# Attention followed by a routed expert layer on one core: rows stored unnormalized and scaled after the gather, and the second search's steps placed by hand between expert 0's row tiles

## The chip, the cores and the metric

One NeuronCore of a Trainium2 chip runs the whole program. The metric is the device time of that core in microseconds (us); lower is better. PE is TensorE, DVE VectorE, ACT ScalarE, POOL GpSimd, SP SyncE (here only a DMA queue).

## The reference

```python
scores = q @ k.T / sqrt(64)                      # q, k, v: [8 batches, 8 heads, 576, 64]
scores = where(scores >= max(scores) - tau, scores, -1e9)
x = softmax(scores) @ v                          # -> 4608 rows of 512
logits = x @ w_gate                              # [4608, 8]
for tok, e in all (token, expert) pairs, largest logit first:
    if tok is unassigned and expert e has < 576 rows: assign tok to e
out[rows of e] = relu(x[rows of e] @ w1[e]) @ w2[e]     # w1 [512, 1024], w2 [1024, 512]
```

## The kernel before, in words

**Attention** (`attention`, L23 to L320) runs pairs of heads through scores, threshold, exponential, transposes and the product with v. It leaves, batch by batch, an unnormalized transposed result XT and a table of 1/denominator (`RD[b]`, one factor for each row and head). A unit `xt_unit(b,c)` (L201) turns one tile of 128 tokens back into rows: four PE transposes into one of two PSUM banks (tile `xo`, L205), an eviction into an SBUF row tile with the factors multiplied in, and a DMA on SP's queue into the DRAM tensor `xrows` [4608, 512], from which the experts gather. Batches 0 and 1 (10 units) are evicted during attention by one DVE multiply (L212). The other 30 units stand in the list `late` and run after attention: in 24 of them ACT copies PSUM to SBUF and POOL multiplies in place (both L218); the six with c = 4 take eight small ACT operations with the factor as scale (L216).

**The router** finds for one expert after another the logit at which it has its 576 rows. A search has seven levels: DVE compares all logits with a set of thresholds (`cmp`), PE counts by nine small matmuls (L420), DVE casts the counts (`cn`), PE folds them (L426), DVE compares with 576 (`jka`), PE reduces (L436 or L441), DVE forms the next thresholds (`E`). Then `pick` chooses the expert (L463), `rank` numbers its rows (L479, L480), and `pack` (L555) makes the list `idx` of its 576 rows: DVE one-hots, nine matmuls (L504), sixteen (L510), DVE `ih` and `idx`. `close` (L517) bars the assigned tokens and the full expert before the next search. All router operations on DVE are recorded through the planner `Vec` and show as line L358. `warm` (L525) emits 20, 4 and 50 matmuls that compute nothing in the first `pack`.

**The experts** (`moe`, L574): for expert number r of the order found, `w1_load` and `w2_load` bring the weights and split each into a high part (ACT, `w1h`, `w2h`) and a rest (DVE, `w1l`, `w2l`); `rows` (L626) issues five indirect DMAs on POOL's queue (L632), for each tile of rows four PE transposes (`turn` in the later kernel; L642), ACT writes `xh` (L645), DVE `xl`. `ffn` (L653) runs layer 1 (L662: eight output blocks f, each with 12 pairs of matmuls), ReLU on ACT (L668) and its split (`H`), layer 2 (L682), and scatters the rows (L689).

**What orders the work.** Each engine executes its list in the order in which the program is recorded. In attention the order is written out; during the first search the loop below puts one late unit about every 1.05 us between the search steps; from the first expert on, `run` steps generators (`packing`, the searches, loads, `rows`) by modelled times while `ffn` emits the matmuls. LATS, GA, RW are such modelled delays: of the search steps, from gather to first transpose, and between the row tiles. Expert 0's rows are transposed before its layer 1; those of experts 1 to 7 are transposed while PE works through layer 2 of the expert before.

```python
    while late:
        if nxt<=at:
            now=R.V.now=nxt; nxt=now+next(ph,1e6)
        else:
            now=at; late.pop(0)()(); at=now+XTY
```

Of the kernel before, what the change touches and what calls it, by code (L numbers as in the profile page):

```python
# [9 lines left out]
F32 = mybir.dt.float32  # L10
# [8 lines left out]
S=576; D=64; HS=288; QK=3*HS+2*S  # L19
PPB=8; LTB=1; VTB=5; HOLD=1; CAPV=3.3; RATE=(2.4,2.4); NBO=2; XAC=(4,); NDEF=4; XTB=4; XTY=1.05; XT0=2.0; XRB=2  # L20


def attention(ctx, tc, qk, vl, tau, wgd, xrows, xts, Lg, nb_batches, ident, swap, R, after_first):  # L23
# [338 lines left out]
class Router:  # L362
# [148 lines left out]
    def compact2(s,ps):  # L511
# [4 lines left out]
        return idx  # L516
    def close(s):  # L517
        V=s.V; wk=s.wk; L=s.L

        cl=wk.tile([128,8],F32,name="cl"); V.tensor_scalar(cl,s.k("w8"),s.m,-FMAX/2,op0=ALU.is_equal,op1=ALU.mult)  # L520
        V.tensor_tensor(L,L,cl.unsqueeze(1).to_broadcast([128,NC_,8]),op=ALU.add)
        u=wk.tile([128,NC_],F32,name="u"); V.tensor_scalar(u,s.sc,BIGS,-FMAX/2,op0=ALU.is_ge,op1=ALU.mult)
        u2=wk.tile([128,NC_],F32,name="u2"); V.scalar_tensor_tensor(u2,s.sc,BIGS+CAP,u,op0=ALU.is_lt,op1=ALU.mult)
        V.tensor_tensor(L,L,u2.unsqueeze(2).to_broadcast([128,NC_,8]),op=ALU.add)
    def warm(s,n):  # L525

        ps=s.ps()
        for i in range(n): s.T.matmul(ps[:,256:384],s.ones,s.tri,start=True,stop=True)
    def phase(s,last=False):
# [24 lines left out]
        held(0.2); s.rank2()  # L554
    def pack(s,first):  # L555
# [11 lines left out]
        yield V.wait() if first else 0.35  # L567
# [4 lines left out]
W1Y=5.0; L2O=(0,4,1,2,3); L2Z=1; HFB=3; RW=[0.2,0.6,1.0,2.0]; LOWP=(0,1); LPF=7; LOWT=1.4; PREPW=1; WLY=(1.0,1.0)  # L572

def moe(ctx,tc,R,start,xrows,w1,w2,out,ident):  # L574
# [10 lines left out]
    def w1_load(r,s):  # L585
        while r>0 and ("w1",r-1) not in done: yield 0.5
# [7 lines left out]
        s["w1h"]=w1p.tile([128,4,F],F32R,name="w1h"); s["w1l"]=w1p.tile([128,4,F],F32R,name="w1l")  # L594
        for k in range(4):
            t=s["w1s",k]
            if r==0:
                A.activation(s["w1h"][:,k],t,AF.Copy)
                while "idx" not in s: yield 0.25
                V.tensor_tensor(s["w1l"][:,k],t,s["w1h"][:,k].bitcast(F32),op=ALU.subtract)  # L600
                yield 1.1; continue
# [6 lines left out]
        done.add(("w1",r))  # L608
    def w2_load(r,s):
# [16 lines left out]
    def rows(r,s):  # L626
        while r>0 and ("x",r-1) not in done: yield 0.5
        order=(4,0,1,2,3) if r<=HALF else range(5)
        for t in order:
            n=128 if t<4 else 64  # L630
            x=wk.tile([128,D],F32,name="xg",bufs=5); s["xg",t]=x
            G.indirect_dma_start(out=x[:n],out_offset=None,in_=xrows,in_offset=IOA(ap=s["idx"][:n,t:t+1],axis=0))  # L632
        s["ei2"]=wk.tile([128,1],I32,name="ei2",bufs=2); G.tensor_copy(s["ei2"],s["ei"])
        done.add(("g",r))
        yield GA[min(r,3)]
        while r>0 and ("l1",r-1) not in done: yield 0.5
        s["xh"]=wk.tile([128,4,576],F32R,name="xh"); s["xl"]=wk.tile([128,4,576],F32R,name="xl")
        for t in order:
            n=128 if t<4 else 64
            ps=pt.tile([128,4,128],F32,name="pt")  # L640
            held[0]+=0.5
            for d in range(4): T.transpose(ps[:,d,:n],s["xg",t][:n,d*128:(d+1)*128],ident[:n,:n])  # L642
            if t<4: xv=lambda n: s[n][:,:,128*t+32*(t//2):128*t+32*(t//2)+128]; pv=ps
            else: xv=lambda n: s[n].rearrange("p k (a b) -> p k a b",a=2)[:,:,:,256:288]; pv=ps[:,:,:64].rearrange("p k (a b) -> p k a b",a=2)
            A.activation(xv("xh"),pv,AF.Copy)  # L645
            yield 0.8
            V.tensor_tensor(xv("xl"),pv,xv("xh").bitcast(F32),op=ALU.subtract)
            done.add(("row",r,t))
            if t==1: done.add(("half",r))
            yield RW[min(r,3)]  # L650
        done.add(("x",r))

    def ffn(r,s):  # L653
        H=wk.tile([128,8,2*CAP],F32R,name="H")
        for f in range(8):
            ps=pf.tile([128,2,512],F32,name="pf")
            for hs in (((0,),(1,)) if r<=HALF and f==0 else ((0,1),)):
                if hs==(1,): yield None
                for k in range(4):
                    for j,(w,x) in enumerate((("w1h","xh"),("w1h","xl"),("w1l","xh"))):  # L660
                        for h in hs:
                            T.matmul(ps[:,h,:HS],s[w][:,k,f*128:(f+1)*128],s[x][:,k,h*HS:(h+1)*HS],  # L662
                                     start=(k==0 and j==0),stop=(k==3 and j==2))
                        if not (k==3 and j==2): yield 0.125*len(hs)
            two=lambda a: a.rearrange("p (a b) -> p a b",a=2)
# [30 lines left out]
    def place():  # L696
        for r in range(8):
# [4 lines left out]
            def steps(g):  # L702
# [11 lines left out]
            yield from steps(start[0] if r==0 else R.phase(r==7))  # L714
            if r==0:
                yield from packing(r,s)
                yield 2.3; R.close(); yield 1.4
            else:
                if r<7: R.close()
                jobs.append([clk[0],packing(r,s)])  # L720
                yield 0.1
    def packing(r,s):
        for d in R.pack(r==0):
            held[0]+=R.pe; R.pe=0.0
            yield d
            V.now=clk[0]
# [88 lines left out]
```

## Time and profile before

| | |
|---|---|
| device time, median of 3 runs | 1034.47 us (1034.33 to 1034.84) |
| the profiled execution | 1035.17 us, span of its instructions 1033.4 us |
| PE busy | 979.6 us (95%), 9104 matmuls |
| DVE / ACT / POOL busy | 776.3 / 640.3 / 324.3 us |
| mean granted PE clock | 0.979 of full speed |
| first search, `idx` of expert 0 written | from 491 us to 535.6 us |
| expert 0, layer 1 complete | 584.6 us |

The busy shares are averages over three parts: attention (to about 490 us), the first search with expert 0's preparation (490 to 560), and the experts (to 1033). Matmuls are pipelined, so two rows of one engine may overlap by a little.

### The profile page before, as it was taken

The page shows a single profiled execution, that of the slowest core. Times are in us where ns is not written, and L with a number is a line of the kernel's source. Part 1 is how long each engine was busy: PE and PEld are TensorE (multiplying, and loading weights), DVE is VectorE, ACT ScalarE, POOL GpSimd, SP SyncE. Part 2 cuts the span into 40 slices and gives each one's busy share as a digit, 9 for nine tenths or more (in the row PEclk, how much of TensorE's full clock was granted, in tenths as well). Part 3 has the DMA queues.
Part 4 walks back from the last instruction along what each step waited for, and adds up shares of the span by engine and source line. Part 5 has one row for each costly group of instructions (what it writes and reads, how often), then busy time and mean ns, then how long its engine had stood idle before and what let it go on. Part 6 is the DMA issues. An engine that isn't in the chain of part 4 may idle for free. (4 is left out here: it accounts for less than half of the span.)

```text
span 1033.4 us, 24026 instructions
## 1 busy us (share of the span) xinstructions
PE 979.6 (95%) x9104; PEld 713.4 (69%) x9104; DVE 776.3 (75%) x2085; ACT 640.3 (62%) x1221; POOL 324.3 (31%) x485
## 2 busy tenths in 40 slices
PE   6999999999999999999668899999999999999996
PEld 3555555555555555555557779788897978889895
DVE  6999999999999999997677677757585676744230
ACT  5898888888888888886544335444352534445340
POOL 2333433333333343331653445312204021231201
PEclk9999999999999999999778999999999999999998
DMA  6222143243432222302463251504325051363101
GB/s 224 99 67 102 61 141 119 98 144 113 153 108 107 89 75 104 108 2 93 168 208 110 82 169 48 196 29 132 129 83 168 14 194 65 126 228 126 41 11 41
DMA packets 35715, 113.03 MB, mean 109 GB/s; under 512 B 4368, under 2 KB 4752, under 8 KB 35088
## 3 DMA queue, kind: packets, MB, share of 16 engines
q1 hardware_dynamic: 28496, 89.47, 24.4%
q0 software_dynamic: 5888, 18.88, 5.9%
q10 hardware_dynamic: 1216, 3.15, 0.9%
q8 instruction: 72, 1.18, 0.5%
q14 instruction: 43, 0.35, 0.1%
HBM read 89.19 MB, written 21.23 MB: 107 GB/s over the span
## 5 line engine op out<-in xcount | busy, mean ns | idle before, releaser
L75 POOL TENSOR_SCALAR nb<-nb,taub 128x1 f32<-128x1 f32 x288 | 147.3, 512 | 296.6 <-DVE z L74 252.4
L74 DVE TENSOR_SCALAR_CACHE_REDUCE z<-sc 128x576 f32<-128x576 f32 x288 | 205.9, 751 | 34.5 <-PE sc L69 33.0
L85 ACT ACTIVATE pp<-z,nb 128x576 f32<-128x576 f32 x256 | 187.4, 773 | 34.6 <-DVE z L74 33.2
L89 DVE SCALAR_TENSOR_TENSOR pp<-z,nb,pp 128x576 f32<-128x576 f32 x256 | 199.8, 812 | 0.3
L682 PE MATMUL pf<-w2h,H 128*128 128x512 f32 x576 | 196.1, 402 | 1.1 <-DVE H L358 1.1
L69 PE MATMUL sc<-qk 64*128 64x288 f32 (+1 forms) x1280 | 181.3, 428 | 6.5 <-DMA qk<-qk_dram 6.2
L144 PE MATMUL xo<-pt,vt 128*64 128x288 f32 x1024 | 151.9, 418 | 0.7 <-ACT xt L151 0.7
L113 ACT ACTIVATE pt<-tb 128x512 f32<-128x512 f32 x256 | 140.1, 594 | 13.8 <-PE tb L98 11.5
L98 PEld LDWEIGHTS tb<-ident,pp 64*128 64x128 f32 x2304 | 85.7, 139 | 71.8 <-ACT pt L113 16.8
L682 PE MATMUL pf<-w2l,H 128*128 128x512 f32 x320 | 128.2, 401 | 0.0
L689 POOL DMA_INDIRECT out_dram<-y,idx x40 | 42.7, 1067 | 265.1 <-ACT y L685 167.9
L682 PEld LDWEIGHTS pf<-w2h,H 128*128 128x128 f32 x576 | 106.3, 188 | 20.0 <-DVE H L358 1.5
L69 PEld LDWEIGHTS sc<-qk 64*128 64x128 f32 (+1 forms) x1280 | 94.3, 179 | 36.4 <-DVE pp L89 9.2
L98 PE MATMUL tb<-ident,pp 64*128 64x64 f32 x2304 | 108.8, 229 | 10.3 <-ACT pt L113 6.2
L662 PE MATMUL pf<-xh,w1h 128*128 128x288 f32 x512 | 113.4, 300 | 1.2 <-ACT xh L645 1.2
L662 PE MATMUL pf<-xh,w1l 128*128 128x288 f32 x512 | 113.7, 300 | 0.0
L662 PE MATMUL pf<-xl,w1h 128*128 128x288 f32 x512 | 113.1, 299 | 0.0
L668 ACT ACTIVATE hf<-pf 128x576 f32<-128x576 f32 x64 | 41.8, 652 | 105.3 <-PE pf L662 94.3
L144 PEld LDWEIGHTS xo<-pt,vt 128*64 128x64 f32 x1024 | 62.5, 136 | 63.5 <-issue 26.5
L685 ACT ACTIVATE y<-pf 128x512 f32<-128x512 f32 x40 | 23.9, 598 | 115.9 <-PE pf L682 99.3
L662 PEld LDWEIGHTS pf<-xh,w1h 128*128 128x128 f32 x512 | 82.9, 189 | 3.7 <-ACT xh L645 1.7
L662 PEld LDWEIGHTS pf<-xl,w1h 128*128 128x128 f32 x512 | 82.6, 189 | 0.2 <-DVE xl L358 0.2
(182 smaller groups left out, 1361.0 us busy)
## 6 DMA issues: line engine op xcount, KB each, us to landing
qk<-qk_dram SPq DMA_DIRECT2D x31, 1008.0 KB, 4.9
w2s<-w_dram SPq DMA_DIRECT2D x32, 512.0 KB, 6.0
w1s<-w_dram SPq DMA_DIRECT2D x28, 512.0 KB, 5.3
vt<-vl_dram SPq DMA_DIRECT2D x32, 320.0 KB, 5.5
xrows<-pp SPq DMA_DIRECT2D x24, 256.0 KB, 2.0
xts<-xt SPq DMA_DIRECT2D x2, 1152.0 KB, 5.2
pt<-xts SPq DMA_DIRECT2D x2, 1152.0 KB
xrows<-xr SPq DMA_DIRECT2D x8, 256.0 KB, 2.1
```

Source lines behind the costliest of these rows:

```text
L69: T.matmul(sc[o,f,:HS], kd["q",h][r,c], kd[k,h][r,:],start=True,stop=True)
L74: V.tensor_scalar(z,SC.pop(t)[:,:,:HS],-0.125,None,op0=ALU.mult,op1=ALU.min,accum_out=nb[:,0:1])
L75: G.tensor_scalar(nb[:,1:2],nb[:,0:1],taub[:,0:1],None,op0=ALU.add)
L85: A.activation(pview(t),ZB[t].rearrange("p a b -> p (a b)"),AF.Exp,bias=NBI[t][:,0:1],scale=-1.0)
L89: V.scalar_tensor_tensor(pv,ZB.pop(t).rearrange("p a b -> p (a b)"),NBI[t][:,1:2],pv,op0=ALU.is_le,op1=ALU.mult,accum_out=den_of(p)[:,p%4, ...
L98: g=slice(64*r,64*r+64); T.transpose(o[:,r],x[g],ident[g,g])
L113: A.activation(PT[p][:,i%2,:,(i//2)*128:(i//2+1)*128].rearrange("p k (r q) -> p r k q",r=2),tb,AF.Copy)
L144: T.matmul(xo[64*h:64*h+64,:HS],v[:,u,64*h:64*h+64],PT[p][:,h,u,q],start=(u==0),stop=False,skip_group_check=True)
L662: T.matmul(ps[:,h,:HS],s[w][:,k,f*128:(f+1)*128],s[x][:,k,h*HS:(h+1)*HS], start=(k==0 and j==0),stop=(k==3 and j==2))
L668: A.activation(hf,ps[:,:,:HS],AF.Relu)
L682: T.matmul(ps[:,0,:],H[:,f,c:c+128],s[w][:,f],start=(f==0 and j==0),stop=e)
L689: G.indirect_dma_start(out=out,out_offset=IOA(ap=s["idx"][:n,t:t+1],axis=0),in_=y[:n],in_offset=None)
```

## The change

1. `xrows` rows become 520 wide: 512 unnormalized values and the row's eight factors. An early unit is a DVE copy and a POOL operation of 128x8 for the factors (both L213 of the new file); a late unit is an ACT copy and an ACT copy of the factors (L215). The POOL multiplies and the small ACT operations of L216 are gone.
2. After the gather, DVE multiplies each row tile in place by its factors (`xg<-xg`); for tile 4 of expert 0 ACT does it in eight operations. The scale of an expert's first tile is recorded at the moment of its first transpose, that of each other tile one tile ahead.
3. For expert 0 the steps of the second search are written by hand between the row tiles; `close` is split into two parts inside `pack` (experts 0 and 1); `w1l` of expert 0 is written after the row tiles in column pieces; its layer 1 takes the products with `w1h` first.
4. The constants LATS, GA and RW change.

```diff
-            if b<nb_batches-NDEF-NBO: V.tensor_tensor(xv,pv,src,op=ALU.mult)
-            elif c in XAC:
...
+            if early:
+                V.tensor_copy(xv,ps[:n]); G.tensor_scalar(fv,src,1.0,0.0,op0=ALU.mult,op1=ALU.add)
             else:
-                A.activation(xv,pv,AF.Copy); G.tensor_tensor(xv,xv,src,op=ALU.mult)
+                A.activation(xv,ps[:n],AF.Copy); A.activation(fv,src,AF.Copy)
             nc.sync.dma_start(xrows[b*S+c*128:b*S+c*128+n,:],xr[:n])
...
         poh=s.onehot(prb); R=s.rank3(hib)
         if first: s.warm(WARM[0])
+        if alone: s.close1()
         yield V.wait()
         held(0.7); s.compact(cps,poh,R)
         if first: s.warm(WARM[1])
+        if alone: s.close2()
...
-LATS=[0.15,0.05,0.4]+[0.6]*5; FIX=(0.125,0.2)
-GA=[7.0,5.5,7.5,9.0]; HALF=1; WARM=[20,4,50]
+LATS=[0.15,0.12,0.25]+[0.35]*5; FIX=(0.125,0.2)
+GA=[5.0,6.0,7.0,7.0]; HALF=1; WARM=[20,4,50]
...
+        if r==0:
+            for k in range(4):
+                A.activation(s["w1h"][:,k],s["w1s",k],AF.Copy); yield 1.1
+            done.add(("w1",0))
+            for a,b in ((0,1),(1,2),(2,4),(4,8)):
+                while ("row",0,1 if a==0 else 3) not in done: yield 0.1
+                o=slice(128*a,128*b)
+                for k in range(4):
+                    V.tensor_tensor(s["w1l"][:,k,o],s["w1s",k][:,o],s["w1h"][:,k,o].bitcast(F32),op=ALU.subtract)
...
+        def scale(t):
...
+            if (r,t)==(0,4):
+                x=s["xg",t][:n]
+                for h in range(8): A.activation(x[:,64*h:64*h+64],x[:,64*h:64*h+64],AF.Copy,scale=x[:,D+h:D+h+1])
+                return
+            v=s["xg",t][:n,:D].rearrange("p (h d) -> p h d",h=8)
+            V.tensor_tensor(v,v,s["xg",t][:n,D:XW].unsqueeze(2).to_broadcast([n,8,64]),op=ALU.mult)
...
+            step(); scale(4); step(); scale(0); turn(4); step(); turn(0); step(); scale(1); low(4); step()
+            turn(1); low(0); step(2); scale(2); yield V.ease()
+            low(1); done.add("ahead"); yield 1.5
+            turn(2); yield 0.8
+            scale(3); low(2); yield 0.7
+            turn(3); low(3)
+            done.add(("x",0)); return
+        scale(order[0])
+        for i,t in enumerate(order):
+            turn(t)
+            if i<4: scale(order[i+1])
+            yield 0.8
+            low(t)
             yield RW[min(r,3)]
...
+                ops=[(k,j) for j in range(3) for k in range(4)] if r==0 else [(k,j) for k in range(4) for j in range(3)]
...
+                    if r==0 and (k,j)==(0,2): yield ("w1l",f)
```

POOL, from the end of attention to expert 0's gathers. Before:

```order
L179 TENSOR_SCALAR lt<-lt 128x64
L218 TENSOR_TENSOR pp<-pp,rd 128x512 x24
L632 DMA xg<-xrows,idx 64x512
```

Now:

```order
L179 TENSOR_SCALAR lt<-lt 128x64
L643 DMA xg<-xrows,idx 64x520
L643 DMA xg<-xrows,idx 128x520 x4
```

POOL has nothing left between attention's last operation and the gathers; the factors of the late units are on ACT's list.

DVE, after expert 0's `idx` (`b` to `cmp` is the start of the second search). Before:

```order
L358 SCALAR_TENSOR_TENSOR idx<-cps,ih 128x5
L358 TENSOR_TENSOR w1l<-w1s,w1h 128x1024 x3
L358 TENSOR_SCALAR cl<-cst,m_8067 128x8
L358 TENSOR_TENSOR Lg<-Lg,cl 128x288
L358 TENSOR_SCALAR u<-scol 128x36
L358 SCALAR_TENSOR_TENSOR u_8259<-scol,u 128x36
L358 TENSOR_TENSOR Lg<-Lg,u_8259 128x288
L358 TENSOR_TENSOR w1l<-w1s,w1h 128x1024
L358 TENSOR_REDUCE b<-Lg 128x36
```

Now:

```order
L355 SCALAR_TENSOR_TENSOR idx<-cps,ih 128x5
L355 TENSOR_REDUCE b<-Lg 128x36
L355 TENSOR_TENSOR q<-Lg,b 128x288
L355 TENSOR_TENSOR q<-q,w8b 128x288
L355 TENSOR_REDUCE qm<-q 128x36
L355 TENSOR_TENSOR oh<-q,qm 128x288
L355 TENSOR_TENSOR cmp<-b,cst 128x1152
L355 CAST cn<-rps 128x32
L355 TENSOR_SCALAR jka,fla<-rps 32x8
L355 TENSOR_TENSOR xg<-xg 128x512
```

The four full `w1l` pieces and `close` have left the stretch behind `idx`; the second search starts there at once, and the first DVE scale follows its second level's start.

DVE, around expert 2's first row tile (`jk`, `E`, `cmp` are steps of the third search after it, `w1l` its weights). Before:

```order
L358 TENSOR_SCALAR jka,fla<-rps 32x8
L358 TENSOR_TENSOR w1l<-w1s,w1h 128x512
L358 SCALAR_TENSOR_TENSOR jk_9687,sm<-cst,rps 128x34
L358 TENSOR_SCALAR E<-cst,sm 128x34
L358 SCALAR_TENSOR_TENSOR E<-cst,sm,E 128x34
L358 TENSOR_TENSOR cmp<-b,E 128x576
L358 TENSOR_TENSOR w1l<-w1s,w1h 128x512
L358 TENSOR_TENSOR xl<-pt,xh 128x4x128
```

Now:

```order
L355 TENSOR_SCALAR jka,fla<-rps 32x8
L355 SCALAR_TENSOR_TENSOR jk_9709,sm<-cst,rps 128x34
L355 TENSOR_SCALAR E<-cst,sm 128x34
L355 SCALAR_TENSOR_TENSOR E<-cst,sm,E 128x34
L355 TENSOR_TENSOR w1l<-w1s,w1h 128x512
L355 TENSOR_TENSOR cmp<-b,E 128x576
L355 TENSOR_TENSOR xg<-xg 128x512 x2
L355 TENSOR_TENSOR xl<-pt,xh 128x4x128
```

The first transposes of a row tile (on PE, which before waited for the gather alone) now stand behind the scale `xg<-xg`, and that behind the operations ahead of it on DVE.

## Rows read from the trace of the kernel before

**Rows 1.** Stretches: us; PE, PEld, DVE, ACT, POOL busy (instructions); PE clock, DMA share, GB/s.

```profile
500.00:510.00 10.00, 6.90 (x53) 5.39 (x54) 7.05 (x16) 4.36 (x13) 4.61 (x4) 0.57 0.44 154
...
498.00:500.00 2.00, 0.00 (x0) 0.00 (x0) 1.93 (x3) 1.63 (x8) 1.68 (x2) 1.00 0.58 219
```

**Rows 2.** Waits of PE, 484 to 537 us: total us, times, longest.

```profile
PE sc L420 <- DVE cmp L358: 7.1, 6, 2.7
```

**Rows 3.** Groups by shape, first search: busy us, mean ns; idle before and its releasers.

```profile
L218 POOL TENSOR_TENSOR pp<-pp,rd 128x512 f32<-128x512 f32 x24 | 27.8, 1175 | 10.9 <-ACT pp L218 10.4 <-DVE cn L358 0.2
...
L216 ACT ACTIVATE pp<-xo,rm 64x64 f32<-64x64 f32 x48 | 10.3, 307 | 2.9 <-PE sc L436 1.5 <-POOL pp L218 0.8 <-PE xo L205 0.6
...
L358 DVE TENSOR_TENSOR cmp<-b,E 128x1152 bf16<-128x1152 f32 x4 | 7.3, 1813 | 0.1
...
L358 DVE TENSOR_TENSOR oh<-q,qm 128x64 bf16<-128x64 bf16 x1 | 0.8, 753 | 0.0
```

**Rows 4.** One line of attention: ns (min/median/max) of its small ACT copies.

```profile
L126 ACT ACTIVATE pl<-tb x32: 203/204/206, 29.0 to 484.3; 64x64 f32<-64x64 f32 x32
```

**Rows 5.** Timeline of DVE, first search: start, us, operation.

```profile
518.01 1.52 DVE L358 TENSOR_TENSOR cmp<-b,E 128x1152 bf16<-128x1152 f32 x1
...
521.43 2.25 DVE L358 TENSOR_TENSOR cmp<-b,E 128x1152 bf16<-128x1152 f32 x1
```

**Rows 6.** Groups of DVE by shape, 610 to 1033 us.

```profile
L358 DVE TENSOR_TENSOR w1l<-w1s,w1h 128x512 fp32r<-128x512 f32 x49 | 33.3, 684 | 6.5 <-ACT w1h L604 6.4
...
L358 DVE TENSOR_TENSOR cmp<-b,cst 128x1152 bf16<-128x1152 f32 x4 | 5.4, 1350 | 0.0
...
L358 DVE TENSOR_TENSOR oh<-q,qm 128x288 bf16<-128x288 bf16 x5 | 2.3, 458 | 0.2
```

**Rows 7.** Timeline of PE, expert 0's row tiles and first layer-1 matmul.

```profile
540.93 0.43 PE L642 MATMUL pt<-ident,xg 64*128 64x64 f32 x4 [1.12 <-ACT w1h L598]
542.30 1.12 PE L642 MATMUL pt<-ident,xg 128*128 128x128 f32 x4 [0.94 <-DMA xg<-xrows,idx]
545.63 1.12 PE L642 MATMUL pt<-ident,xg 128*128 128x128 f32 x4 [2.22 <-DVE xl L358]
547.43 0.61 PE L662 MATMUL pf<-xh,w1h 128*128 128x288 f32 x1 [0.69 <-ACT xh L645]
```

**Rows 8.** Timeline of ACT: the first and the last of expert 0's eight ReLUs.

```profile
554.72 0.66 ACT L668 ACTIVATE hf<-pf 128x576 f32<-128x576 f32 x1 [2.88 <-PE pf L662]
...
584.84 0.65 ACT L668 ACTIVATE hf<-pf 128x576 f32<-128x576 f32 x1 [3.44 <-PE pf L662]
```

**Rows 9.** Waits of PE, 560 to 640 us.

```profile
PE pf L682 <- DVE H L358: 1.1, 1, 1.1
PE pt L642 <- DMA xg<-xrows,idx: 1.1, 3, 0.6
```

**Rows 10.** Timeline of DVE, second search: a first level's end, and beside expert 1's transposes.

```profile
554.10 0.26 DVE L358 SCALAR_TENSOR_TENSOR jk<-cst,rps 128x34 f32<-128x34 f32 x1 [1.39 <-PE rps L441]
...
554.97 0.76 DVE L358 TENSOR_TENSOR cmp<-b,E 128x576 bf16<-128x576 f32 x1
...
606.51 0.69 DVE L358 TENSOR_TENSOR w1l<-w1s,w1h 128x512 fp32r<-128x512 f32 x1
607.11 0.75 DVE L358 TENSOR_TENSOR cmp<-b,E 128x576 bf16<-128x576 f32 x1
607.78 0.68 DVE L358 TENSOR_TENSOR xl<-pt,xh 128x512 fp32r<-128x512 f32 x1
```

**Rows 11.** Waits of PE, 610 to 1033 us: first and last of four.

```profile
PE rps L420 <- DVE cmp L358: 0.7, 2, 0.5
...
PE rps L436 <- DVE jka L358: 0.3, 1, 0.3
```

**Rows 12.** Timeline of PE in expert 1's layer 2, around expert 2's transposes.

```profile
665.58 0.63 PE L682 MATMUL pf<-w2h,H 128*128 128x512 f32 x2
666.04 0.40 PE L682 MATMUL pf<-w2l,H 128*128 128x512 f32 x1
```

More of the change, by code (lines that the diff above doesn't have):

```diff
@@ L524, in close @@
         V.tensor_tensor(L,L,u2.unsqueeze(2).to_broadcast([128,NC_,8]),op=ALU.add)
+    def close(s): s.close1(); s.close2()
     def warm(s,n):
@@ L554, in phase, with pack @@
         held(0.2); s.rank2()
-    def pack(s,first):
+    def pack(s,first,alone):
         V=s.V; hib,prb=s.hib,s.prb; cps=s.cp()
@@ L566, in pack @@
         if first: s.warm(WARM[2])
-        yield V.wait() if first else 0.35
+        yield V.wait() if alone else 0.35
         s.idx=s.compact2(cps)
-LATS=[0.15,0.05,0.4]+[0.6]*5; FIX=(0.125,0.2)
-GA=[7.0,5.5,7.5,9.0]; HALF=1; WARM=[20,4,50]
-W1Y=5.0; L2O=(0,4,1,2,3); L2Z=1; HFB=3; RW=[0.2,0.6,1.0,2.0]; LOWP=(0,1); LPF=7; LOWT=1.4; PREPW=1; WLY=(1.0,1.0)
+LATS=[0.15,0.12,0.25]+[0.35]*5; FIX=(0.125,0.2)
+GA=[5.0,6.0,7.0,7.0]; HALF=1; WARM=[20,4,50]
+W1Y=5.0; L2O=(0,4,1,2,3); L2Z=1; HFB=3; RW=[0.2,0.5,0.8,1.0]; LOWP=(0,1); LPF=7; LOWT=1.4; PREPW=1; WLY=(1.0,1.0)
 def moe(ctx,tc,R,start,xrows,w1,w2,out,ident):
@@ L585, in w1_load @@
     def w1_load(r,s):
-        while r>0 and ("w1",r-1) not in done: yield 0.5
+        while r>0 and ("w1a",r-1) not in done: yield 0.5
         q=nc.scalar if r==0 else nc.sync
@@ L594, in w1_load @@
         s["w1h"]=w1p.tile([128,4,F],F32R,name="w1h"); s["w1l"]=w1p.tile([128,4,F],F32R,name="w1l")
+        if r==0:
[7 more added lines that the diff above has]
+                    V.tensor_tensor(s["w1l"][:,k,o],s["w1s",k][:,o],s["w1h"][:,k,o].bitcast(F32),op=ALU.subtract)
+                    if a>1: yield 0.9 if a<4 else 2.0
+                for f in range(a,b): done.add(("w1l",f))
+            done.add(("w1a",0))
+            return
         for k in range(4):
             t=s["w1s",k]
[L597 to L601, printed above, removed]
             for c in range(2):
@@ L607, in w1_load @@
                 yield WLY[1]
-        done.add(("w1",r))
+        done.add(("w1",r)); done.add(("w1a",r))
     def w2_load(r,s):
@@ L615, in w2_load @@
         yield 5.0
-        while ("w1",r) not in done or (r==0 and ("x",0) not in done) or (r>0 and ("l2",r-1) not in done): yield 0.5
+        while ("w1a",r) not in done or (r==0 and ("x",0) not in done) or (r>0 and ("l2",r-1) not in done): yield 0.5
         s["w2h"]=wk.tile([128,8,D],F32R,name="w2h"); s["w2l"]=wk.tile([128,8,D],F32R,name="w2l")
@@ L630, in rows @@
             n=128 if t<4 else 64
-            x=wk.tile([128,D],F32,name="xg",bufs=5); s["xg",t]=x
+            x=wk.tile([128,XW],F32,name="xg",bufs=5); s["xg",t]=x
             G.indirect_dma_start(out=x[:n],out_offset=None,in_=xrows,in_offset=IOA(ap=s["idx"][:n,t:t+1],axis=0))
@@ L634, in rows @@
         done.add(("g",r))
+        def scale(t):
+            n=128 if t<4 else 64
+            if (r,t)==(0,4):
+                x=s["xg",t][:n]
+                for h in range(8): A.activation(x[:,64*h:64*h+64],x[:,64*h:64*h+64],AF.Copy,scale=x[:,D+h:D+h+1])
+                return
+            v=s["xg",t][:n,:D].rearrange("p (h d) -> p h d",h=8)
+            V.tensor_tensor(v,v,s["xg",t][:n,D:XW].unsqueeze(2).to_broadcast([n,8,64]),op=ALU.mult)
+        if r==0:
+            step0=R.phase(); R.ahead=step0
+            for _ in range(3): next(step0)
         yield GA[min(r,3)]
@@ L637, in rows, with parts, turn, low @@
         s["xh"]=wk.tile([128,4,576],F32R,name="xh"); s["xl"]=wk.tile([128,4,576],F32R,name="xl")
-        for t in order:
+        def parts(t):
+            ps=s["xps",t]
+            if t<4: return (lambda n: s[n][:,:,128*t+32*(t//2):128*t+32*(t//2)+128]),ps
+            return (lambda n: s[n].rearrange("p k (a b) -> p k a b",a=2)[:,:,:,256:288]),ps[:,:,:64].rearrange("p k (a b) -> p k a b",a=2)
+        def turn(t):
             n=128 if t<4 else 64
-            ps=pt.tile([128,4,128],F32,name="pt")
+            ps=pt.tile([128,4,128],F32,name="pt"); s["xps",t]=ps
             held[0]+=0.5
             for d in range(4): T.transpose(ps[:,d,:n],s["xg",t][:n,d*128:(d+1)*128],ident[:n,:n])
[L643 to L646, printed above, removed]
+            xv,pv=parts(t); A.activation(xv("xh"),pv,AF.Copy)
+        def low(t):
+            xv,pv=parts(t)
             V.tensor_tensor(xv("xl"),pv,xv("xh").bitcast(F32),op=ALU.subtract)
@@ L649, in rows, with step @@
             if t==1: done.add(("half",r))
+        if r==0:
+            def step(n=1):
+                for _ in range(n): next(R.ahead)
+            step(); scale(4); step(); scale(0); turn(4); step(); turn(0); step(); scale(1); low(4); step()
[11 more added lines that the diff above has]
+            low(t)
             yield RW[min(r,3)]
@@ L657, in ffn @@
             for hs in (((0,),(1,)) if r<=HALF and f==0 else ((0,1),)):
[L658 to L664, printed above, removed]
+                if hs==(1,): yield ("x",r)
+                ops=[(k,j) for j in range(3) for k in range(4)] if r==0 else [(k,j) for k in range(4) for j in range(3)]
+                for i,(k,j) in enumerate(ops):
+                    w,x=(("w1h","xh"),("w1h","xl"),("w1l","xh"))[j]
+                    if r==0 and (k,j)==(0,2): yield ("w1l",f)
+                    for h in hs:
+                        T.matmul(ps[:,h,:HS],s[w][:,k,f*128:(f+1)*128],s[x][:,k,h*HS:(h+1)*HS],start=(i==0),stop=(i==11))
+                    if i<11: yield (0.25 if (r,f)==(0,0) else 0.125)*len(hs)
             two=lambda a: a.rearrange("p (a b) -> p a b",a=2)
@@ L713, in steps @@
                     jobs.append([clk[0],w1_load(r,s)]); jobs.append([clk[0]+0.1,w2_load(r,s)])
-            yield from steps(start[0] if r==0 else R.phase(r==7))
-            if r==0:
+            yield from steps(start[0] if r==0 else R.ahead if r==1 else R.phase(r==7))
+            if r<2:
                 yield from packing(r,s)
-                yield 2.3; R.close(); yield 1.4
+                while "ahead" not in done: yield 0.1
             else:
@@ L722, in packing @@
     def packing(r,s):
-        for d in R.pack(r==0):
+        for d in R.pack(r==0,r<2):
             held[0]+=R.pe; R.pe=0.0
@@ L742, in moe @@
         for d in ffn(r,st[r]):
-            while d is None and ("x",r) not in done:
-                now+=0.25; run(now)
-            if d is None: continue
+            if type(d) is tuple:
+                while d not in done:
+                    now+=0.25; run(now)
+                continue
             held[0]=0.0; now+=d; run(now); now+=held[0]; clk[0]=now
@@ L784, in build @@
         dr=ctx.enter_context(tc.tile_pool(name="dr",bufs=1,space=bass.MemoryType.DRAM))
-        xrows=dr.tile([8*S,512],F32,name="xrows")
+        xrows=dr.tile([8*S,XW],F32,name="xrows")
         xts=dr.tile([8,128,4,S],F32,name="xts")
```

21 lines of the change are left out of this document (10 added, 11 removed).

## The prediction

> **What bounds the kernel now.** Three views, in this order. The busy table of the page first: PE works 979.6 of 1033.4 us, so the end of the program is the end of PE's list, and a change counts only where it alters a wait or the clock of PE. Then the stretches of 10 and 2 us: outside attention and the experts there is one weak place, the first search and expert 0's preparation, about 490 to 550 us. From 498 to 500 PE runs nothing, and the stretch of 500 to 510 has a granted clock of 0.57 [rows 1]. Then PE's waits there: 7.1 us for `cmp` alone [rows 2]; the engine that it waits for is DVE. Behind 610 us the waits are four kinds, from 0.7 us down to 0.3 [rows 11]: the experts run with PE full, and whatever delays PE there is added to the end undiminished.
>
> **Why DVE is late in the search.** While POOL multiplies rows (24 x 1175 ns) DVE's operations are longer than the same shapes elsewhere: `cmp` of 128x1152 takes 1813 ns on average, against 1350 ns in the experts; a small `oh` of 128x64 takes 753 ns, where one four times as wide takes 458 [rows 3, 6]. One pair shows it within the search: 1.52 us at 518.01, 2.25 us at 521.43 [rows 5]. I added the excess over eleven kinds of DVE operation, the first and last being those two (4 x 0.46 and 0.3): 9.9 us.
>
> **The change part by part.**
>
> (a) *The search without POOL.* The 24 multiplies and 48 small ACT operations (10.3 us of ACT [rows 3]) go. A late unit keeps its ACT copy and gains one of 128x8; that shape is not in the trace. Nearest are the 64x64 ACT copies at 0.204 us [rows 4] (lower end) and the 64x64 with a scale at 0.307 [rows 3] (upper end); I take 0.20, 30 x 0.20 = 6 us less the 10.3 that go. ACT had room, and a unit is due about every 1.05 us with one copy of 0.6: nothing on the path. The chain compare, count, fold, reduce, threshold is then free of stretched operations. Step by step with the clean level (518.01 to 521.43, 3.42 us [rows 5]) the pick comes 9.9 us earlier, the same as the excess. Moving `close` into `pack` puts some 0.2 us ahead of `idx`: **-9.7 us** at `idx` (535.6 before). It needs the clock to stay up: the clock fell after PE had run nothing for 2 us at 498 to 500 [rows 1], waiting for `jk`, `E`, `E` and `cmp`. Undisturbed these end 0.87 + 0.76 = 1.6 us after `jk` starts [rows 10], with a unit's transposes beside them.
>
> The ten early units trade a DVE multiply for a DVE copy and give POOL ten small operations; PE in attention waits for neither. Zero; without that cover a late factor delays its own unit's store alone, and nothing gathers from `xrows` for 300 us.
>
> (b) *Expert 0.* Before, from `idx` at 535.6: PE took the first two gathered tiles at 540.93 and 542.30, the second as its gather landed, 6.7 us after `idx`; the first layer-1 matmul came at 547.43 and the first ReLU at 554.72, 19.1 us after `idx`; the last of eight ReLUs at 584.84 [rows 7, 8]. The full `w1l` pieces no longer stand ahead, so the 2.2 us wait for `xl` [rows 7] goes; but each row tile now waits for its scale, and the search steps come between the tiles. An ACT scale of tile 4 is eight times about 0.2 = 1.7 us. By hand, with the gathers 1.4 us apart as those two and so landing from 5.2 to 10.7 us after `idx`: scale of tile 4 to 7.0, first layer-1 matmul at 12.1, dense from 14.4, first block done at 20.9: +1.8. A block is 12 pairs of 576 columns, a pair 0.26 us at the rate of layer 2 (512 columns in 0.23 [rows 12]); seven blocks need 22 us, plus 2.6 of search steps and 0.4 of waits, 25.0; before they took 584.84 - 554.72 = 30.1 [rows 8], since the second search stood among them. 25.0 - 30.1 + 1.8 = **-3.3**. The wait of 1.1 us for `H` [rows 9] loses most of its cause with the search steps: **-0.8**.
>
> (c) *The scaled rows.* 39 DVE multiplies of 128x512 by a broadcast factor are new. No row has one; the nearest is `w1l` of the same shape and two SBUF operands at 0.684 us [rows 6] (lower end), the farther end POOL's own multiply at 1.175 [rows 3]. I take 0.68. DVE is not the bound, so 26 us more of it cost nothing by themselves. What costs is the order: the first tile's scale is recorded at the moment of its transposes, behind whatever DVE has then, and PE waits in order. For expert 2 the listing shows it: PE reduces the flag, six layer-2 matmuls follow, then the transposes. A matmul comes every 0.23 us (two in 666.04 - 665.58 [rows 12]), so PE is there after 1.5 us. DVE has `jk`, `E`, `E` (0.87 [rows 10]), `w1l` (606.51 to 607.11, 0.60), `cmp` (607.11 to 607.78, 0.67 [rows 10]), the scale 0.68, and handing over about 0.1: 2.9 to 3.1. Wait: 1.5. Worked out likewise for each expert from its listing:
> - expert 1: 1.45 at the first tile (counts, `cn`, `w1l`, scale), 0.6 and 1.7 at later tiles behind `xl`, `w1l` and the search, less the 1.1 that its gathers cost before [rows 9]: +2.7;
> - expert 2: 1.6, and 0.8 at later steps: +2.4;
> - expert 3: the same chain, but ten matmuls between flag and transposes: 0.75; expert 4: the chain and six matmuls, 1.7; expert 5: nothing between the counts and the transposes, so `cn`, the scale and handing over, 1.3; expert 6: `pack`'s one-hots (3.6 us of DVE by hand) against eight matmuls, 1.8;
> - expert 7, with no search beside it: 0.
>
> Together **+10.6**. With the scale at POOL's price and ten such places it would be +15.6.
>
> (d) *Wider rows.* Gathers and writes carry 1.6% more bytes; the gather of expert 0 is waited for (0.94 us [rows 7]). By the bytes alone 1.6% of the 6.7 us, 0.1; zero to 0.2, and I take **+0.2**. A rule of the Trainium skill speaks against it: the page "DMA: Bandwidth & Descriptors", section "How a descriptor splits into AXI transactions", says that a row that isn't a multiple of 256 B, or does not start on one, costs extra transactions. For rows of 2080 B that is an estimate of up to an eighth more; by it five gathers 1.4 us apart would end some 0.8 us later and the sum would be -2.4 instead of -3.0. No run so far shows such rows.
>
> Sum: -9.7 - 3.3 - 0.8 + 10.6 = -3.2, with 0.2 for the rows **-3.0**. The profiled execution took 1035.17, 0.7 above the median of the runs shown; 1032.2 for it means **1031.5** for the median.
>
> **The rivals.**
> - *The scales find DVE idle* (chance 0.15). If DVE is ahead of PE at every tile, (c) is nothing: -13.6, 1020.9. For it: DVE waits for others between its groups in the experts (6.4 us before `w1l` alone [rows 6]). Against: the chains of experts 2, 4, 5 begin at a matmul of PE itself, a few matmuls ahead of the transposes, so no lead of DVE helps.
> - *The clock falls in the search all the same* (0.17). The units run in the same order and PE still pauses between levels. At half clock the transposes and counts stretch and I get only 5.5 of the 9.7: +4.2 on the forecast, 1035.7.
> - *The slower side: the scales of later tiles are late too* (0.18). In experts 2 to 6 the second to fifth tiles' scales stand behind `xl`, `w1l` and search steps as in expert 1. Were each such expert to cost what expert 1 does (3.7), (c) is 5 x 3.7 + 2.7 = 21.2 and the time 1042.1. It decides from waits above 13.6 us on; for it speaks the closer spacing of tiles (RW from 1.0 and 2.0 to 0.8 and 1.0) and of search steps, against it that these scales are recorded one tile ahead.
>
> **How the numbers follow.** The forecast has 0.50; its own range, from the hand-made waits (8 to 15) and the search (-8 to -11), is 1026.5 to 1036.5. About 0.2% (2.07 us) is what a measurement of this kernel can tell from no change: faster is below 1032.4, slower above 1036.5. Faster: 0.35 of the forecast, 0.15 of the first rival, 0.02 of the second: 0.52. The same: 0.11 + 0.08 + 0.02 = 0.21. Slower: 0.04 + 0.07 + 0.16 = 0.27. Range 1020 to 1038: it holds the forecast and the first two rivals and leaves out the third.
>
> **What would show it.** The list of rows of expert 0 written at about 526 instead of 535.6; `cmp` of 128x1152 in the search near 1.4 us; no stretch of 500 to 520 with a clock near 0.5. Layer 1 of expert 0 over at about 572. In the experts a new kind of PE wait, transposes for `xg` written by DVE, of some 10 us in about ten places, largest in expert 1. If that wait is absent, or far above 14 us, or the granted clock in the search is half again, the forecast is wrong in that step.

## The result, and the profile after

| | before | after |
|---|---|---|
| median of 12 runs each, one comparison | 1034.88 us (1032.65 to 1036.56) | 1037.34 us (1035.50 to 1038.68) |
| ratio after / before | | 1.0024, 95% interval 1.0017 to 1.0032 |
| profiled execution, span | 1035.17, 1033.4 us | 1037.63, 1035.8 us |
| `idx` of expert 0 written | 535.6 us | 522.9 us |
| last ReLU of expert 0 | 584.84 us | 572.09 us |
| idle PE time listed against transposes of experts 1 to 7, 573 us to the end | 1.1 us (three gathers) | 14.5 us |

The kernel became slower by 0.24%, where 0.29% faster was forecast; the time lies within the range, the sign is wrong. A repeat in another comparison gave 1.0005 (0.9996 to 1.0015), see e6_again: the two intervals do not overlap, and by the second the change cannot be told from none. Neither is the gain that was forecast.

The front half did what the forecast says, and more. The stretches and the group of `cmp` of the changed kernel (columns as in [rows 1] and [rows 3]):

```profile
490.00:500.00 10.00, 8.29 (x92) 6.65 (x93) 6.31 (x29) 8.06 (x27) 0.00 (x0) 1.00 0.82 291
500.00:510.00 10.00, 7.88 (x91) 6.04 (x88) 5.94 (x17) 7.54 (x24) 0.00 (x0) 1.00 0.78 276
```

```profile
L355 DVE TENSOR_TENSOR cmp<-b,E 128x1152 bf16<-128x1152 f32 x4 | 5.4, 1358 | 0.1
L355 DVE TENSOR_TENSOR oh<-q,qm 128x64 bf16<-128x64 bf16 x1 | 0.2, 225 | 0.0
```

POOL is silent, `cmp` is down from 1813 to 1358 ns, the small `oh` from 753 to 225, and from 500 to 510 us the granted clock is 1.00 where it was 0.57. The list of rows is 12.7 us earlier, and so is the last ReLU of expert 0:

```profile
572.09 0.65 ACT L713 ACTIVATE hf<-pf 128x576 f32<-128x576 f32 x1 [2.30 <-PE pf L708]
```

Behind it the lead is lost again. Start of each expert's last ReLU, after minus before: expert 0 -12.7, expert 1 -12.9, expert 2 -11.0, expert 3 -10.4, expert 4 -8.4, expert 5 -2.2, expert 6 +1.4, expert 7 +2.4 us. The waits of PE from 573 us to the end (total, times, longest; two more of 0.2 us follow):

```profile
PE pt L669 <- issue: 8.4, 6, 2.4
PE pt L669 <- DVE xg L355: 5.8, 4, 3.0
PE pf L727 <- DVE H L355: 0.9, 1, 0.9
PE pt L669 <- PE rps L423: 0.3, 1, 0.3
```

L669 are the transposes of gathered rows. Before, such waits behind 573 us were the 1.1 us of [rows 9], and [rows 11] held small waits alone (0.7 us in all and less). All 14.5 us stand before transposes whose rows DVE has just scaled ("issue" is where the profile names no releaser; the timeline shows the scale ending there, below). Expert 5 loses most. DVE, POOL and PE of the changed kernel around its fourth tile:

```profile
848.37 1.19 POOL L734 DMA_INDIRECT out_dram<-y,idx  x1 [6.07 <-ACT y L730]
...
848.92 1.96 DVE L355 SCALAR_TENSOR_TENSOR sm<-sm 128x1 f32<-128x1 f32 x1
...
849.59 1.27 POOL L737 TENSOR_TENSOR y<-y,z 64x512 f32<-64x512 f32 x1
850.92 0.30 DVE L355 TENSOR_SCALAR E<-cst,sm 128x34 f32<-128x34 f32 x1
851.13 0.68 DVE L355 TENSOR_TENSOR xg<-xg 128x512 f32<-128x512 f32 x1
...
851.92 0.30 PE L669 MATMUL pt<-ident,xg 128*128 128x128 f32 x1 [2.35 <-issue]
```

A DVE operation of 128x1, 0.16 us elsewhere, lasts 1.96 us: it ends when POOL's addition ends (849.59 + 1.27 = 850.86). The scale queues behind it, and PE behind the scale. After the two waits of this expert (2.96 and 2.35 us) the clock falls, for the only time between 544 us and the last 6 us of the program (there it is low in the kernel before too):

```profile
850.00:852.00 2.00, 0.08 (x1) 0.11 (x2) 1.96 (x4) 0.00 (x0) 0.85 (x1) 1.00 0.40 156
852.00:854.00 2.00, 2.00 (x10) 1.43 (x10) 1.79 (x4) 0.60 (x1) 1.27 (x1) 0.83 0.00 0
854.00:856.00 2.00, 2.00 (x8) 1.43 (x8) 1.39 (x4) 0.38 (x1) 0.00 (x0) 0.50 0.34 72
856.00:858.00 2.00, 2.00 (x9) 1.58 (x8) 0.00 (x0) 0.00 (x0) 0.00 (x0) 0.81 0.01 2
```

Counting the missing share of each stretch as lost, that is 2 x (0.17 + 0.50 + 0.19) = 1.7 us more, an estimate. All listed waits behind expert 0's last ReLU sum to 15.8 us after, 14.5 of them for transposes, and to 4.1 before ([rows 9, 11]); 11.7 and 1.7 make 13.4 of the 15.1 us lost from there to the end (-12.7 to +2.4). The other 1.7 are in no wait. Part of them has a place: from the first to the last ReLU of expert 7, beside which no search runs, the changed kernel takes 22.40 us (978.69 to 1001.09) and the kernel before 22.22 (976.49 to 998.71). All runs below with rows of 512 take 22.2 there, and all with rows of 520 take 22.4, those without scales too. Over seven experts that would be 1.3 us, an estimate; what slows these matmuls, which do not read the gathered rows, no run settles.

### The profile page after: what moved, and what is told of

It is laid out like the page before. It is cut to its first block, busy times and chain, and to the rows that moved or that the text cites. A ratio compares the mean times of both kernels' runs of the same rounds, so it can differ in the third digit from the quotient of the medians.

```text
span 1035.8 us, 24039 instructions
## 1 busy us (share of the span) xinstructions
PE 977.4 (94%) x9104; PEld 710.9 (69%) x9104; DVE 791.3 (76%) x2136; ACT 637.9 (62%) x1217; POOL 299.1 (29%) x471
## 4 chain that ended last, share of the span: by engine, by line
PE 71%; DVE 11%; ACT 9%; issue 6%; DMA 3%; another core or an unknown queue 0%; ACTq 0%; DVEq 0%; POOLq 0%; POOL 0%; SPq 0%
PE pf L708 19%; PE pf L727 17%; PE xo L144 10%; PE sc L69 8%; PE tb L98 8%; ACT pp L85 4%; ACT pt L113 2%; PE xo L149 2%; DVE z L74 2%; DVE pp L89 2%; PE pt L669 2%; ACT pt L115 2%; DVE cmp L355 1%; PE xo L205 1%; PE xo L176 1%
## 5 line engine op out<-in xcount | busy, mean ns | idle before, releaser
L98 PE MATMUL tb<-ident,pp 64*128 64x64 f32 x2304 | 108.8, 229 | 10.6 <-ACT pt L113 6.2
L708 PE MATMUL pf<-xh,w1h 128*128 128x288 f32 x512 | 110.9, 303 | 0.1
L708 PE MATMUL pf<-xh,w1l 128*128 128x288 f32 x512 | 110.9, 302 | 0.0
L708 PE MATMUL pf<-xl,w1h 128*128 128x288 f32 x512 | 110.1, 302 | 0.7 <-DVE xl L355 0.7
```

The costliest lines, as they stand in the source:

```text
L98: g=slice(64*r,64*r+64); T.transpose(o[:,r],x[g],ident[g,g])
```

## The experiments

Theory A: the gain is the silent POOL; the loss is PE waiting, in its own order, for scales that are recorded too late on DVE. Rivals: the wider rows and the new constants (B), no room on DVE (C), a search bound by something else (D), the hand-placed order (E). Each run's ratio is to the kernel before on the same chip.

**e1_noscale.** The scales of experts 1 to 7 are left out.

```diff
         def scale(t):
-
+            if r>0: return
             n=128 if t<4 else 64
```

> The changed kernel without the DVE scales of experts 1 to 7 (their rows stay unnormalized; expert 0's are scaled). Theory A: the loss behind expert 0 is PE waiting in its order for the scales, 14.6 us of waits and some 2 us of lower clock that they bring in expert 5, so the kernel ends near 1037.3 - 16.6 + 1 (the gathers' own landing) = 1022, and transposes of xg wait for almost nothing behind 580 us. Rival B: the wider rows and the closer planner constants cost as such: then 1030 or more, with the transposes still waiting, for gathers.

Measured: 1024.12 us, ratio 0.9889 (0.9872 to 0.9905). Of waits for transposes 0.3 us is left behind 560 us, gathers of wide rows and new constants included. B falls: without the scales nearly the whole front gain reaches the end. Whether it is their work or their place that costs, the next run tells.

**e2_ahead.** The same scales, earlier.

```diff
-        yield GA[min(r,3)]
+        if r==0: yield GA[0]
+        else:
+            yield GA[min(r,3)]-2.0
+            scale(order[0])
+            yield 2.0
+            scale(order[1])
...
-        scale(order[0])
         for i,t in enumerate(order):
             turn(t)
-            if i<4: scale(order[i+1])
+            if i<3: scale(order[i+2])
```

> The changed kernel with the scales of experts 1 to 7 recorded earlier: the first two tiles' 2 us ahead of the first transposes, each other two tiles ahead. Theory A: the waits for scales fall from 14.6 us to 3 to 5 and the clock stays up: 1025 to 1028, faster than both. Rival C (DVE has no room, whatever the order): waits move to xl and the search steps, 1034 to 1038.

Measured: 1023.40 us, 0.9880 (0.9863 to 0.9896). Its waits from 560 us on, the first four of six:

```profile
PE pt L674 <- DVE xg L355: 1.1, 1, 1.1
PE rps L423 <- DVE cn L355: 1.1, 1, 1.1
PE pt L674 <- issue: 0.9, 1, 0.9
PE pf L731 <- DVE H L355: 0.9, 1, 0.9
```

All 35 scales of experts 1 to 7 are there and cost PE 2.0 us instead of 14.5, less than expected. C falls. This version beats both kernels.

**e3_oldconst.** The changed kernel with the old constants.

```diff
-LATS=[0.15,0.12,0.25]+[0.35]*5; FIX=(0.125,0.2)
-GA=[5.0,6.0,7.0,7.0]; HALF=1; WARM=[20,4,50]
+LATS=[0.15,0.05,0.4]+[0.6]*5; FIX=(0.125,0.2)
+GA=[7.0,5.5,7.5,9.0]; HALF=1; WARM=[20,4,50]
```

(and RW as before).

> The changed kernel with LATS, GA and RW of the kernel before. Theory A: the place of the scales against the search steps changes by chance, the sum of waits for them stays 8 to 18 us: 1032 to 1040. Rival B: the constants are the cause of the loss: 1026 or less.

Measured: 1042.06 us, 2 us above the range expected, 1.0053 (1.0033 to 1.0072). Transposes wait 6.2 + 5.1 us; the rows are now so late that layer 1 waits too (1.9 and 1.5 us), and the clock falls at 732 and 864 us. The new constants help; they are not the loss.

**e4_before_nomul.** The kernel before, its late units copied by ACT and not normalized.

```diff
-            elif c in XAC:
...
             else:
-                A.activation(xv,pv,AF.Copy); G.tensor_tensor(xv,xv,src,op=ALU.mult)
+                A.activation(xv,pv,AF.Copy)
```

> The kernel before without the POOL multiplies and the small ACT operations of the 30 late units (an ACT copy only; their rows stay unnormalized, and nothing scales them). Theory A: the POOL multiply is what stretched DVE in the first search: idx of expert 0 at about 523 to 526 instead of 535.6, and 1023 to 1026 in all. Rival D (the search is bound by its own chain or by ACT): idx at 532 or later, 1031 or more.

Measured: 1022.84 us, 0.9876 (0.9860 to 0.9893); `idx` at 523.2 us.

```profile
500.00:510.00 10.00, 7.91 (x94) 6.25 (x93) 6.06 (x17) 6.67 (x12) 0.00 (x0) 1.00 0.77 270
...
L354 DVE TENSOR_TENSOR cmp<-b,E 128x1152 bf16<-128x1152 f32 x4 | 5.4, 1358 | 0.1
```

With nothing else of the change, `cmp` and the clock are those of the changed kernel. D falls. The 13 us to the kernel before are what normalizing costs there.

**e8_only216.** Only the small ACT operations go, the POOL multiplies stay.

```diff
-                for j in range(4):
-                    for h in range(2):
-                        A.activation(xv[:,j,h],pv[:,j,h],AF.Copy,scale=...
+                A.activation(xv,pv,AF.Copy)
```

> The kernel before with its 24 POOL multiplies, but an ACT copy in place of the small ACT operations of L216 (the six tiles with c = 4 stay unnormalized). Theory A: the POOL multiplies alone stretch DVE, so at most 1 to 3 us are gained: 1032 to 1035. Rival D (the small ACT operations hold up PSUM banks and so the search): half or more of the 13 us of e4_before_nomul, 1029 or less.

Measured: 1032.96 us, 0.9987 (0.9977 to 0.9996): 0.13% of the 1.24% of e4.

```profile
L356 DVE TENSOR_TENSOR cmp<-b,E 128x1152 bf16<-128x1152 f32 x4 | 7.3, 1822 | 0.1
```

With POOL's multiplies there, `cmp` is stretched; the multiplies are the cause of that. They are not all of the lead: `idx` comes at 532.6 us here, 3.0 us earlier than in the profile of the kernel before, of the 12.4 in e4. So some 9.4 us go with the multiplies and 3.0 with the small ACT operations, by one profile each; in the time of the program the latter are worth 1.4 us.

**e5_noadd and e6_again.** The changed kernel without POOL's addition, and the changed kernel unaltered, in one comparison. The addition left out is that of tile 4's residual product to its sum.

```diff
-                G.tensor_tensor(y5[0:64],y5[0:64],z,op=ALU.add); store(4,y5,64)
+                store(4,y5,64)
```

> The changed kernel without POOL's addition of the two halves of tile 4 (L737; half of that tile's layer-2 sum is left out). Theory A: in experts 5 and 6 a DVE operation that stands beside this addition lasts 2 us instead of 0.2 to 0.7 and makes PE wait 2.4 and 1.1 us for a scale; without it these waits fall below 0.7 each and the clock stays up in expert 5: 1032 to 1034.5. Rival: those operations wait for something else, and it stays within 1 us of the changed kernel.

> The changed kernel once more, unaltered, for a second profile. If the long wait of expert 5 (PE 3.0 us for the first scale, DVE idle 2.6 us before a cast) belongs to its place in the program, it is there again at over 2 us; if it was an accident of that execution, it is below 1.5 us. 1036.5 to 1039.

Measured: 1030.98 us, 0.9964 (0.9950 to 0.9978), against 1035.19, 1.0005 (0.9996 to 1.0015): 4.2 us for one addition of 1.3 us per expert. Both came out faster than expected, by 1.0 and 1.3 us. Waits of e6_again, 573 us to the end, then of e5_noadd:

```profile
PE pt L669 <- DVE xg L355: 6.8, 6, 1.7
PE pt L669 <- issue: 5.3, 4, 2.4
```

```profile
PE pt L669 <- DVE xg L355: 6.8, 6, 1.7
PE pt L669 <- issue: 2.4, 3, 1.2
```

The same `sm` of expert 5, in e6_again and in e5_noadd (there with the scatter that POOL runs beside it in both runs):

```profile
847.40 1.96 DVE L355 SCALAR_TENSOR_TENSOR sm<-sm 128x1 f32<-128x1 f32 x1
```

```profile
846.13 1.19 POOL L734 DMA_INDIRECT out_dram<-y,idx  x1 [3.99 <-ACT y L730]
...
846.69 0.16 DVE L355 SCALAR_TENSOR_TENSOR sm<-sm 128x1 f32<-128x1 f32 x1
...
847.88 0.63 PE L669 MATMUL pt<-ident,xg 128*128 128x128 f32 x4 [0.55 <-issue]
```

In expert 6 it is the scale of the fifth tile itself that lasts longer beside the addition (916.43 to 917.72 in the changed kernel); without the addition it takes 0.68 us:

```profile
916.07 2.20 DVE L355 TENSOR_TENSOR xg<-xg 64x512 f32<-64x512 f32 x1
```

The wait of 2.35 us is 0.55, one of 1.14 us in expert 6 is gone, and the clock stays up in expert 5. The other reading (those operations wait for something else) falls. The long wait at expert 5's first tile, which I had expected of e6_again at over 2 us if it belonged to the program, was 0.88. In the first profile DVE stood idle there with its input ready (first row), in this one only for PE (second):

```profile
843.37 0.19 DVE L355 CAST cn<-rps 128x32 fp32r<-128x32 f32 x1 [2.64 <-remote]
```

```profile
841.85 0.19 DVE L355 CAST cn<-rps 128x32 fp32r<-128x32 f32 x1 [0.57 <-PE rps L417]
```

So the profiled execution of the first comparison holds 2.1 us that this one does not. Whether the other eleven runs of that median hold them too is not shown; the two medians, 1037.34 and 1035.19, differ by 2.2 us.

**e10_firstonly and e11_lateronly.** Half of e2_ahead each.

```diff
+        if r==0: yield GA[0]
+        else:
+            yield GA[min(r,3)]-2.0
+            scale(order[0])
+            yield 2.0
...
-        scale(order[0])
         for i,t in enumerate(order):
```

```diff
-        scale(order[0])
+        scale(order[0]); scale(order[1])
...
-            if i<4: scale(order[i+1])
+            if i<3: scale(order[i+2])
```

> The changed kernel with only the first tile's scale of experts 1 to 7 recorded 2 us ahead of its transposes; the others one tile ahead as in the changed kernel. Theory A: the seven waits at first tiles (7.4 us in e6_again) go, the later ones (5.1 us, 3.5 of them beside POOL's addition) stay, with or without their fall of the clock: 1026.5 to 1030.

> The changed kernel with the first tile's scale at the moment of its transposes as it is, and every other tile's two tiles ahead. Theory A: the waits at first tiles stay or grow, 7 to 10 us, the later ones fall below 1.5 us and the clock stays up: 1028 to 1032.

Measured: 1022.70 us, 0.9891 (0.9875 to 0.9908), and 1028.37, 0.9946 (0.9930 to 0.9963). e11 came as expected, with 6.8 us of waits at six first tiles; e10 did better than expected. With the first scale early, the later tiles' waits nearly vanish as well (1.4 us; the 1.1 us are expert 6's first tile. The rows of e10 from 573 us on):

```profile
PE pt L673 <- issue: 1.4, 4, 0.8
PE pt L673 <- DVE xg L355: 1.1, 1, 1.1
```

So the later waits were mostly a consequence: "one tile ahead" is enough once the first tile is ahead too. e11 shows what the place alone does while the hold stays. There the same `sm` of expert 5 is held beside POOL's addition as before, but behind all five scales, and PE's wait in that expert's later tiles is 1.14 us instead of 2.35. It stands at the fifth tile, whose scale had ended 3.2 us earlier; what still queues behind `sm` is an `xl`:

```profile
844.65 1.98 DVE L355 SCALAR_TENSOR_TENSOR sm<-sm 128x1 f32<-128x1 f32 x1
```

**e7_ahead_warm.** e2_ahead with a block of matmuls that compute nothing ahead of expert 0's second transposes.

```diff
-            step(); scale(4); step(); scale(0); turn(4); step(); turn(0); step(); scale(1); low(4); step()
+            step(); scale(4); step(); scale(0); turn(4); step(); R.warm(26); turn(0); step(); scale(1); low(4); step()
```

> e2_ahead with 26 matmuls that compute nothing put ahead of expert 0's second transposes, where PE waits 1.6 us for a gather and the clock falls. If the idle stretch is what lets the clock fall, it stays up behind it and layer 1 of expert 0 ends 2 to 4 us earlier: 1019.5 to 1022. If the later waits (cmp, counts, xl) bring it down just the same, within 1 us of e2_ahead.

Measured: 1022.68 us, 0.9888 (0.9872 to 0.9905): nothing gained over e2_ahead. The clock was already at 0.50 from 528 us, ahead of the block, which so ran at the lower level. Behind it the clock was up from 534 to 538 us (0.89 and 0.97), and after waits of 0.58 and 1.46 us for `jka` and `xl` it was at 0.50 again: the later waits bring it down, as the second expectation says. Whether a block placed earlier would pay was not tried.

**e9_oldorder and e12_ahead_again.** The kernel before with unnormalized rows, early scales and the new constants (all but GA of expert 0, which stays at 7.0), but the old order of expert 0 and of the second search; and e2_ahead once more beside it. The core of e9's edit to the kernel before, beside the change's own new eviction and scale:

```diff
-        yield GA[min(r,3)]
+        yield GA[min(r,3)]-2.0
+        scale(order[0])
+        yield 2.0
+        scale(order[1])
...
             A.activation(xv("xh"),pv,AF.Copy)
+            if i<3: scale(order[i+2])
             yield 0.8
```

> The kernel before with the unnormalized rows, the scales recorded early as in e2_ahead and the new constants, but expert 0 and the second search in the order of the kernel before (no steps placed by hand, close and w1l where they were, layer 1 in the old order of products). Theory A: the hand-placed order gives nothing; from idx to the last ReLU of expert 0 it takes 48 to 50 us (48.2 in e2_ahead), 1022 to 1026. Rival E (placing by hand is worth the 3.3 us of the prediction): 51 us or more, 1026 or more.

> e2_ahead once more, unaltered, beside e9 to e11 on one chip: ratio to the kernel before 0.987 to 0.990; the idle stretch of DVE of 2.2 us before a cast in expert 5 (836.6 us) not there again if it belonged to that execution.

Measured: 1023.87 us, 0.9904 (0.9886 to 0.9922), and 1022.48, 0.9883 (0.9866 to 0.9899). From `idx` to expert 0's last ReLU the old order takes 48.2 us, the hand-placed one 48.9 here. E falls: it is not the 3.3 us forecast. Whether the placing by hand is worth anything is open: the two intervals overlap, but each run of e9 is slower than each of e12 (1023.12 at the least, 1022.83 at the most). The medians differ by 1.4 us, and in e9 PE waits 3.2 us with transposes behind 573 us, in e12 1.9. The idle stretch of 2.2 us before a cast that e2_ahead had in expert 5 is not there again.

## Why the prediction was wrong, step by step

- **(a) The search without POOL: right in kind, undersized.** Forecast -9.7 us at `idx`, measured -12.7; e4 and e8 show that POOL's multiplies are most of the cause, and that the small ACT operations, which I had put at "nothing on the path", are some 3 us of it. Levels took about 3.25 us, not the 3.42 of the one that I called clean [rows 5]: its `cmp` of 1.52 was itself stretched; and the search began 0.6 us earlier. The clock stayed up to the pick, so the second rival did not happen.
- **(b) Expert 0: wrong.** The first ReLU came 21.2 us after `idx` (forecast 20.9), but the other seven blocks took 572.09 - 544.14 = 28.0 us instead of 25.0. PE's waits in them are 0.7 us; with 22 us of blocks some 5 us are left for the search steps, which I had put at 2.6. From `idx` to the last ReLU: 49.2 us before and after, so 0 instead of -3.3. The errors of (a) and (b) cancel, by luck: -13.0 forecast, -12.7 measured at that ReLU. The -0.8 for the wait for `H` did not come either: it is 0.9 us, where it was 1.1.
- **(c) The scaled rows: the step that decided the sign.** From the last ReLU of expert 0 to the end the forecast has -0.8 + 10.6 + 0.2 = +10.0, the kernels differ by +15.1; with -12.7 ahead of it the one makes a gain, the other a loss. The +10.6 are net of the gathers' 1.1. Waits by expert, forecast / recorded profile / e6_again: expert 1 3.7 / 2.4 / 2.4; expert 2 2.4 / 1.7 / 1.7; expert 3 0.75 / 0.4 / 0.4; expert 4 1.7 / 1.3 / 1.3; expert 5 1.3 / 5.3 / 3.2; expert 6 1.8 / 2.9 / 2.9; expert 7 0 / 0.6 / 0.6. The chains counted from the listing were too high by 0.4 to 1.3 us in each of experts 1 to 4. Experts 5 and 6 are where the step failed: I counted their first tiles alone, and the fourth of expert 5 and the fifth of expert 6 wait on DVE operations that POOL's addition holds up (2.35 and 1.14 us); in expert 5 the clock falls after it (1.7 us). I had put both at nothing. In the recorded run came 2.1 us of an idle DVE. That addition is the very effect on which (a) rests, read in the search and not looked for in the experts, where the trace of the kernel before has it too, in an operation for which PE does not wait (0.22 us in the search of the changed kernel):

```profile
614.79 1.42 DVE L358 TENSOR_SCALAR hb<-cst,sm 128x5 bf16<-128x5 f32 x1
614.86 1.31 POOL L692 TENSOR_TENSOR y<-y,z 64x512 f32<-64x512 f32 x1
```

- **(d) The wider rows: small, not settled.** In e1_noscale the transposes hardly wait for gathers. Of expert 0 the second gather was in use 2.4 us after its issuing instruction on POOL ended in the three profiles with narrow rows (before, e4, e8); with wide ones, where DVE's scale is the first to use it and not PE, 2.6 us in seven profiles, 2.9 in e10 and 3.3 in the changed kernel and in e12. A cost like the 0.8 us estimated from the Trainium skill's "DMA: Bandwidth & Descriptors" ("How a descriptor splits into AXI transactions") is not ruled out by that difference, but no run changed the width alone. In experts 1 to 7 a gather's cost is hidden. Not forecast are the 0.18 us by which layer 1 of expert 7 is longer wherever rows are wide.
- **The rivals.** The slower one came true in part: it named late scales of later tiles, but in all experts and by the search's own operations. The first rival, scales that PE never waits for, is what e2_ahead, e10 and e12 make of the same change: 0.988 to 0.989, -12 us, near the -13.6 that I had put on it; near in the sum only, for in e2_ahead `idx` is 12.1 us earlier, not 9.7, and expert 0 1.0 us shorter, not 3.3. My argument against it, that the chains begin at a matmul just ahead of the transposes, held only for the order as written: the scale needs nothing from that chain and could be put in front of it.

## What to carry to other kernels

When a step moves to another engine, and an engine that works through its list in order waits for it there, count what stands ahead of it on its new engine, and if its input is there earlier, record it ahead of that queue: here 2 us for the first tile decided between 0% and -1.1%. When an engine pair is seen to stretch each other in one stage, look for the same pair in every stage in which the change puts one of them on the critical path. And compare with the time of the kernel with the moved work left out (e1, e4): it tells at once whether the work or its place costs.

## What the runs showed of the hardware that I had not expected

- A DVE operation can last many times its length beside one of POOL: `sm` took 1.96 us instead of 0.16, ending with POOL's 1.27 us addition, and 4.2 us of the program hung on that addition. The Trainium skill, "SBUF — State Buffer", "Who interferes with whom", says that a DVE operation with two SBUF inputs shares a read port with a GpSimd operation that reads SBUF, and that whoever holds it blocks the other altogether. The `cmp` and `sm` rows agree with it. The stretched `sm` starts while POOL still runs the scatter of 1.19 us. In e5_noadd it starts at the same place, 0.56 us into that scatter, and lasts 0.16 us, so the scatter alone does not hold it. Why the hold begins 0.66 us ahead of the recorded start of the addition these rows do not tell.
- In the middle of dense work the granted clock fell to 0.50 after waits of PE of 2.96 and 2.35 us in expert 5, in e6_again after 0.88 and 2.35; after the waits of up to 1.71 us elsewhere in both profiles it did not. In e5_noadd, with 0.88 and 0.55, it stayed at 1.00. The longest wait does not decide alone: in e3_oldconst it fell at 864 us after waits of 0.28 and 0.68.
- DVE stood idle for about 2 us with its input ready (843.37 in the recorded profile, 836.62 in e2_ahead), at the same cast of expert 5, and not there in e5 to e7 or e10 to e12. In e1_noscale it was idle for 3.25 us at another place of the search (before the operation at 644.17), where its input had been ready for 2.4. The cause stays open.
